# A parallel attention and MLP kernel: the first 512 tokens' second products of two pairs in one sum, and a subtract in two halves

## The chip, the cores and the metric

The kernel runs on one core of one Trainium2 chip. The metric is device time in microseconds (us) of one execution. An execution of the kernel before is 713.65 us (median of three runs, 713.02 to 713.98).

## The reference

`x` has 2048 tokens of 640 features. The output is the sum of three branches, two of which work on the layer-normed input:

```python
xn = _layernorm(x, axis=-1)
return x + _A_ref(xn, A_wqkv, A_w_phi, A_wo) + _B_ref(xn, B_w1, B_b1, B_w2, B_b2)
# A: 32 heads of 20; softmax features of q and k, linear attention, @ wo
# B: y = _layernorm(x); h = _gelu(y @ w1 + b1)   (F = 1728);  h @ w2 + b2
```

The change lies in branch B, the MLP.

## The kernel before, in words

All data is float32. For TensorE each operand is split exactly into a high and a low part of type float32r, and a product is three matmuls (`mm3`, L69 to L72): high by high (L70), high by low (L71), low by high (L72). The weights are the first operand, so L72 needs the low part of the weights and L71 the low part of the tokens or of the hidden layer.

Tokens are handled in four blocks of 512 (block 0 to 3), features in 5 chunks of 128 (`KC`), the hidden layer in 14 chunks of 128, which are taken in 7 pairs. For a pair and a block, `Mlp.passes` makes the *first products* (y by w1, per chunk of the pair, 5 `mm3` each), GELU and the split of the hidden layer, and then the *second products*: for each of 5 output chunks `m`, two `mm3` (one for each chunk of the pair) into a bank of PSUM, and one addition on VectorE of this bank into `acc[b]` (L329 for pair 0, which adds the bias b2 too; L331 for the others). The bank comes from `self.po`, which goes round banks 5, 6 and 7; bank 3 and 4 (`self.px`) are for side work. TensorE can write a bank again only when VectorE's addition has read it.

Work that is not the MLP's is put between the matmuls by hand. Each `mm3` ends with `self.tick()`, which runs the steps that are due (`self.after(ticks, step)`) and takes one step of a generator `mlp.beside`. On VectorE, ScalarE (ACT), GpSimd (POOL) and TensorE the order of the instructions is the order in which the code issues them (`manual_schedule`) in the two stages that matter here; each engine works its own queue in order.

The **first stage** (L523 to L696): pair 0's first products of block 0 are made in half blocks while the tokens still arrive. Then come the first products of pair 1 in block 0, the second products of pair 0 (`p00`) and those of pair 1 (`p10`); after `p10`'s third and fourth addition `products` (L640) puts a batch of four small matmuls (shown as eight L644) between. Beside it `next_y` (L651) splits w2 of pair 1 (L671: ACT makes the high part at L61, GpSimd the low part at L64) and makes the normalized tokens of block 1: GpSimd subtracts the mean (L680), VectorE scales (L682), ACT makes the high part (L684), VectorE the low part (L686). The first products of block 1 need these.

The **later stage** (L1358 to L1383): for blocks 2 and 3 the pairs 1 to 5 use a scheme of seven products instead of eight (`cross`), which needs sums of weight blocks. `sums` (L380) makes them on GpSimd, 768 columns (`s`), and `splits` (L406) splits them into high and low: ACT copies `s` (L392), and one tick later VectorE subtracts (L393, 128x768). The five uses of it are called the first to the fifth split here; the second to fifth are issued in the loop at L1377 to L1380, while `second` (L334) makes the second products of block 2. The low part is used by the next pair's `cross`. On VectorE's queue stand there also: `second`'s additions into `acc` (L342), the low part of the hidden layer (L461), the attention's additions (L1228) that free banks 3 and 4 for the attention's products (L1214, L1215), and shuffles (L1263). GpSimd has subtracts for the other weights (L393, 128x640), for the attention's features (L1208) and products for the attention's quotients (L1265).

Of the kernel before, what the change touches and what calls it, by code (L numbers as in the profile page):

```python
# [9 lines left out]
F32R = mybir.dt.float32r  # L10
AF = mybir.ActivationFunctionType
ALU = mybir.AluOpType
# [3 lines left out]
P = 128  # L16
S, D, F, H, DH = 2048, 640, 1728, 32, 20
KC = D // P
# [28 lines left out]
def f(ap):  # L47
    return ap.bitcast(F32)
# [3 lines left out]
def tile_kernel(ctx: ExitStack, tc: tile.TileContext, x, xT, wkT, wqT, wv, wphi, wo, w1, b1, w2, b2,  # L52
                ident, mmask, emask, vsel, out):
    nc = tc.nc
# [14 lines left out]
    def mm3(ps, lh, ll, rh, rl, first, last, **kw):  # L69
        nc.tensor.matmul(ps, lh, rh, start=first, stop=False, **kw)  # L70
        nc.tensor.matmul(ps, lh, rl, start=False, stop=False, **kw)  # L71
        nc.tensor.matmul(ps, ll, rh, start=False, stop=last, **kw)  # L72
# [6 lines left out]
    b2t = cp.tile([P, KC], F32, name="b2t")  # L79
# [18 lines left out]
    acc = [None] * NB  # L98
# [21 lines left out]
    def mtile(i, dtype=F32):  # L120
        return mp.tile([P, 2, D if i < 5 else 512], dtype, name=f"m{i}")
# [92 lines left out]
    class Mlp:  # L214
# [74 lines left out]
        def passes(self, g, b, ws, hid=None):  # L289
# [27 lines left out]
            for m in range(KC):  # L317
# [13 lines left out]
                    nc.vector.tensor_tensor(acc[b][:, m, :], pw, acc[b][:, m, :], op=ALU.add)  # L331
                yield

        def second(self, g, b, w, hid):  # L334

            for m in range(KC):
                pw = self.po()
                ms = slice(m * P, (m + 1) * P)
                for j, (hh, hl) in enumerate(hid):
                    mm3(pw, w[:, 2 * j, ms], w[:, 2 * j + 1, ms], hh, hl, j == 0, j == 1)  # L340
                    self.tick()
                nc.vector.tensor_tensor(acc[b][:, m, :], pw, acc[b][:, m, :], op=ALU.add)  # L342
                yield

        def fetch_pair(self, g, second):

            r1 = rp.tile([P, D], F32, name="r1")
            r2 = rp.tile([P, D], F32, name="r2")
            self.raw[g, second] = r1, r2
            for c, r in ((2 * g, r1), (2 * g + 1, r2)):  # L350
                n = min(P, F - c * P)
                if second:
                    for o in range(0, P, n):
                        nc.sync.dma_start(r[o:o + n, :], w2[c * P:c * P + n, :])
                else:
                    nc.sync.dma_start(r.rearrange("p (c f) -> p c f", f=P)[:, :, 0:n], w1[c, :, :, 0:n])
# [49 lines left out]
        def splits(self, g):  # L406

            raw, sums = self.weights(g)
            r1, r2 = self.raw.pop((g, False))
            s = self.raw.pop((g, "s")).rearrange("p i q f -> p (i q f)")  # L410
            return [lambda: self.split(raw[0][:, 0], raw[0][:, 1], r1), lambda: self.split(sums[:, 0], sums[:, 1], s, nc.vector),
                    lambda: self.split(raw[1][:, 0], raw[1][:, 1], r2)]

        def cross(self, g, bs, before, later):
# [102 lines left out]
    mlp = Mlp((0, 1, 2, 3), ((0, 2), (1, 3)))  # L517

    def finish(p):
        for _ in p:  # L520
            pass
# [6 lines left out]
    wc, parts, dmas = {}, {}, {}  # L528
# [8 lines left out]
    gts = mtile(4)  # L537
    hid = [mtile(2 * j + 1, F32R) for j in range(2)]
    hid = [(h[:, 0, :512], h[:, 1, :512]) for h in hid]
# [67 lines left out]
    next(rows1)  # L607
    for c in range(2):
        parts[c][1](nc.vector)
    p00 = mlp.passes(0, 0, [wc[0], wc[1]], hid)  # L610
    next(p00)

    rs = ExitStack()
    fp = rs.enter_context(tc.tile_pool(name="prep", bufs=2, reuse_waits="tile"))
# [25 lines left out]
    def products(us, raw):  # L640
        ps = mlp.px()
        for u, (n, g, i) in enumerate(us):
            nh = 6 if g < 5 else 4
            nc.tensor.matmul(ps[:, u * nh * DF:(u + 1) * nh * DF], raw[:nh * DH, u * P:(u + 1) * P], wpt[:nh * DH, g, :nh, 1:],  # L644
                             start=True, stop=True)
        return us, ps
# [40 lines left out]
            yield  # L687

    mlp.beside = next_y()
    p10 = mlp.passes(1, 0, [wc[2], wc[3]])  # L690
    next(p10)
    finish(p00)
    for m, _ in enumerate(p10):
        if m in (2, 3):
            first_done.append(products(jobs[0][m - 2], first_raws[m - 2]))
    finish(mlp.beside)  # L696
# [154 lines left out]
    for g in range(2, 7):  # L851
        for b in range(2):
            if b == 0:
                ws, wn = wn, []
# [162 lines left out]
    for t, i in [(t, i) for t in range(14) for i in range(4)] + TAIL:  # L1017
        if (t, i) in ((4, 0), (8, 0)):
            b = t // 4 + 1
# [33 lines left out]
        if (t, i) == (11, 0):  # L1053
            mlp = Mlp((0, 3, 2, 1), ((1, 2), (0, 3)))
# [16 lines left out]
    def pairs(w1t, w2t):  # L1071

        return [(*(w1t[:, 2 * j + p].rearrange("p (c f) -> p c f", f=P) for p in range(2)), w2t[:, 2 * j], w2t[:, 2 * j + 1])
                for j in range(2)]

    ws = pairs(w1t, w2t)
# [256 lines left out]
    at = {}  # L1333
# [36 lines left out]
    for g in range(1, 6):  # L1370
        w2t, later = gathered(g)
        hid, more = mlp.cross(g, (2, 3), before, later)
# [19 lines left out]
    ws = pairs(w1t, w2t)  # L1392
# [17 lines left out]
    for b in range(NB):  # L1410
        oh, ol = at[b].oh, at[b].ol
        for m in range(KC):
            ms = slice(m * P, (m + 1) * P)

            for cols in [slice(0, 512)] if (b, m) != (NB - 1, KC - 1) else [slice(0, 256), slice(256, 512)]:
                pw = pw_()[:, cols]
# [72 lines left out]
```

## Time and profile before

| | |
|---|---|
| three runs | 713.02, 713.65 and 713.98 us |
| the profiled execution | 713.46 us, of which its span (first to last instruction) is 711.6 us |
| TensorE (PE) | 703.8 us busy, 99% |
| weight loads (PEld) | 592.2 us |
| VectorE (DVE) | 514.0 us, 72% |
| GpSimd (POOL) | 421.4 us, 59% |
| ScalarE (ACT) | 342.0 us, 48% |
| granted TensorE clock | 1.000 over the span |
| moved by DMA | 106.56 MB, 149 GB/s over the span |

Rows in time order give the start in us from the span's start, the duration in us, the engine, the line of the kernel, the operation, what it writes and reads by the program's names, the shape, and in brackets the idle time of the engine before it and what ended it. A matmul's row is longer than the distance to the next one's start, since matmuls are pipelined. Names lose their numbers in the profile: `bank` is any PSUM bank, `m` any of the scratch tiles, `w` any weight tile.

### The profile page before, as it was taken

To read this page: it belongs to the slowest core of one execution; us is meant where nothing else is said; L and a number is where in the kernel's file an instruction comes from. 1 tells how busy PE (TensorE), PEld (TensorE's weight loads), DVE (VectorE), ACT (ScalarE), POOL (GpSimd) and SP (SyncE) were. 2 spreads that over 40 slices of the span, in tenths; PEclk is the share of its full clock that TensorE was granted. 3 is DMA by queue.
4 is the path that set the end of the run, shared out by engine and by line. 5 is a ranking of instruction groups with operands and counts; after the bars stand their busy time and mean duration, and the time that the engine had idled before them with its cause. 6 is when DMAs were issued, how large, how long until landed. Compare 5 with 4: busy or idle time off the path is not lost. (4 is left out here: it accounts for less than half of the span.)

```text
span 711.6 us, 9745 instructions
## 1 busy us (share of the span) xinstructions
PE 703.8 (99%) x3381; PEld 592.2 (83%) x3381; DVE 514.0 (72%) x821; ACT 342.0 (48%) x563; POOL 421.4 (59%) x360
## 2 busy tenths in 40 slices
PE   9999999999999999999999999999999999999998
PEld 7878888888888888888888888888887878888886
DVE  7777755988754788788888878657769695784622
ACT  6434554444334545545544546367665766450100
POOL 3521314577245997898787879468679787540400
PEclk9999999999999999999999999999999999999999
DMA  9823643485621228236401609964355568446222
GB/s 325 288 72 109 193 121 98 155 266 172 214 105 74 93 75 245 70 110 199 99 0 32 159 1 349 227 191 127 115 162 153 164 187 296 164 127 214 84 80 74
DMA packets 65767, 106.56 MB, mean 150 GB/s; under 512 B 7462, under 2 KB 31814, under 8 KB 63838
## 3 DMA queue, kind: packets, MB, share of 16 engines
q1 hardware_dynamic: 65414, 105.93, 46.5%
q8 instruction: 26, 0.43, 0.2%
q14 instruction: 23, 0.19, 0.1%
q10 hardware_dynamic: 304, 0.01, 0.0%
HBM read 71.37 MB, written 34.55 MB: 149 GB/s over the span
## 5 line engine op out<-in xcount | busy, mean ns | idle before, releaser
L906 PE MATMUL bank<-wkh,y 128*128 128x512 f32 (+1 forms) x480 | 139.5, 364 | 0.0
L70 PE MATMUL bank<-y,w 128*128 128x512 f32 (+1 forms) x294 | 114.2, 389 | 0.0
L71 PE MATMUL bank<-y,w 128*128 128x512 f32 (+1 forms) x294 | 113.7, 387 | 0.0
L72 PE MATMUL bank<-y,w 128*128 128x512 f32 (+1 forms) x294 | 113.6, 386 | 0.0
L64 POOL TENSOR_TENSOR w<-r,w 128x640 fp32r<-128x640 f32 x32 | 52.2, 1645 | 96.0 <-ACT w L61 67.0
L70 PE MATMUL bank<-m,w 128*128 128x512 f32 x260 | 102.3, 394 | 1.1 <-DVE acc L331 0.8
L71 PE MATMUL bank<-m,w 128*128 128x512 f32 x260 | 101.3, 390 | 0.9 <-DVE m L461 0.9
L72 PE MATMUL bank<-m,w 128*128 128x512 f32 x260 | 101.3, 390 | 0.0
L906 PEld LDWEIGHTS bank<-wkh,y 128*128 128x128 f32 x480 | 87.5, 188 | 13.3
L906 PE MATMUL bank<-wkl,y 128*128 128x512 f32 (+1 forms) x240 | 87.4, 364 | 0.0
L70 PEld LDWEIGHTS bank<-y,w 128*128 128x128 f32 x294 | 55.2, 188 | 11.7 <-issue 0.4
L72 PEld LDWEIGHTS bank<-y,w 128*128 128x128 f32 x294 | 55.2, 188 | 11.3
L71 PEld LDWEIGHTS bank<-y,w 128*128 128x128 f32 x294 | 55.2, 188 | 10.9
L942 ACT ACTIVATE m<-m,rs_all 128x1280 f32<-128x1280 f32 x32 | 43.7, 1365 | 42.9 <-POOL m L941 42.8
L70 PEld LDWEIGHTS bank<-m,w 128*128 128x128 f32 x260 | 48.8, 188 | 11.9 <-DVE acc L331 1.0
L944 DVE TENSOR_REDUCE sm<-m 128x64 f32<-128x1280 f32 x32 | 47.4, 1481 | 15.0 <-ACT m L942 14.8
L71 PEld LDWEIGHTS bank<-m,w 128*128 128x128 f32 x260 | 48.8, 188 | 11.1 <-DVE m L461 1.4
L906 PE MATMUL bank<-w,y 128*128 128x512 f32 x240 | 57.4, 391 | 0.0
L72 PEld LDWEIGHTS bank<-m,w 128*128 128x128 f32 x260 | 48.8, 188 | 10.2
L941 POOL TENSOR_TENSOR m<-m,mx 128x640 f32<-128x640 f32 (+2 forms) x48 | 44.4, 939 | 19.2 <-DVE mx L930 19.2
L331 DVE TENSOR_TENSOR acc<-bank,acc 128x512 f32<-128x512 f32 x70 | 46.9, 683 | 11.1 <-PE bank L72 5.9
L906 PEld LDWEIGHTS bank<-w,y 128*128 128x128 f32 x240 | 44.4, 188 | 8.5
(184 smaller groups left out, 1447.2 us busy)
## 6 DMA issues: line engine op xcount, KB each, us to landing
r<-in_w SPq DMA_DIRECT2D x52, 320.0 KB
e<-e SPq DMA_DIRECT2D x40, 256.0 KB
e<-acc SPq DMA_DIRECT2D x52, 160.0 KB
acc<-in_xT SPq DMA_DIRECT2D x4, 1280.0 KB
t<-t SPq DMA_DIRECT2D x8, 512.0 KB
tf<-t SPq DMA_DIRECT2D x2, 1536.0 KB
xb<-in_x SPq DMA_DIRECT2D x8, 320.0 KB
t<-in_x SPq DMA_DIRECT2D x8, 320.0 KB
```

The costliest lines, as they stand in the source:

```text
L64: eng.tensor_tensor(lo, src, f(hi), op=ALU.subtract)
L70: nc.tensor.matmul(ps, lh, rh, start=first, stop=False, **kw)
L71: nc.tensor.matmul(ps, lh, rl, start=False, stop=False, **kw)
L72: nc.tensor.matmul(ps, ll, rh, start=False, stop=last, **kw)
L331: nc.vector.tensor_tensor(acc[b][:, m, :], pw, acc[b][:, m, :], op=ALU.add)
L906: nc.tensor.matmul(ps, lh[:, kc, c], rh[:, kc], start=n == 0, stop=n == 3 * KC - 1)
L941: subs[n, t] = nc.gpsimd.tensor_tensor(ep[:, s], a, b, op=ALU.subtract)
L942: exps[n, t] = nc.scalar.activation(e, e, AF.Exp, scale=rs_all[:, t:t + 1])
L944: nc.vector.tensor_reduce(sm, e.rearrange("p s (h f) -> p (s h) f", f=DH), axis=AX, op=ALU.add)
```

## The change

Two edits. First, block 0's second products of pairs 0 and 1 are no longer two passes with ten additions. A new method `firsts` makes pair 1's first products, and `seconds` sums both pairs in one bank per output chunk, with one addition (with bias) each, five in all. Pair 0's products for the first three chunks go to the three banks first; then, chunk by chunk, pair 1's products are added in the same bank. The two batches of `products` stay behind the third and fourth addition. Second, in `splits` the subtract that makes the low part of the sums is issued in two halves of 384 columns, one tick and three ticks after ACT's copy.

```diff
+        def firsts(self, g, b, ws):
+            self.turn ^= 1
+            hid, gts = [], mtile(4)
+            for j, w in enumerate(ws):
+                hs = mtile(self.hid[self.turn][j], F32R)
+                hid.append((hs[:, 0, :512], hs[:, 1, :512]))
+                self.first(g, j, b, w, gts[:, j, :512], *hid[-1])
+            return hid
+
+        def seconds(self, b, *pairs):
+            def products(m, n):
+                ws, hid = pairs[n]
+                ms = slice(m * P, (m + 1) * P)
+                for j, (w, (hh, hl)) in enumerate(zip(ws, hid)):
+                    mm3(pw[m], w[2][:, ms], w[3][:, ms], hh, hl, (n, j) == (0, 0), (n, j) == (1, 1), skip_group_check=True)
+                    self.tick()
+
+            pw = [self.po() for _ in range(3)]
+            for m in range(3):
+                products(m, 0)
+            for m in range(KC):
+                if m > 2:
+                    pw.append(self.po())
+                    products(m, 0)
+                products(m, 1)
+                nc.vector.scalar_tensor_tensor(acc[b][:, m, :], pw[m], b2t[:, m:m + 1], acc[b][:, m, :], op0=ALU.add, op1=ALU.add)
+                yield
...
-            return [..., lambda: self.split(sums[:, 0], sums[:, 1], s, nc.vector),
+            def sum_parts():
+                nc.scalar.activation(sums[:, 0], s, AF.Copy)
+                for i, ticks in enumerate((1, 3)):
+                    at = slice(3 * P * i, 3 * P * (i + 1))
+                    self.after(ticks, lambda at=at: nc.vector.tensor_tensor(sums[:, 1, at], s[:, at], f(sums[:, 0, at]), op=ALU.subtract))
+
+            return [..., sum_parts,
...
-    p00 = mlp.passes(0, 0, [wc[0], wc[1]], hid)
-    next(p00)
+    mlp.turn ^= 1
...
-    p10 = mlp.passes(1, 0, [wc[2], wc[3]])
-    next(p10)
-    finish(p00)
-    for m, _ in enumerate(p10):
+    hid = [hid, mlp.firsts(1, 0, [wc[2], wc[3]])]
+    for m, _ in enumerate(mlp.seconds(0, ([wc[0], wc[1]], hid[0]), ([wc[2], wc[3]], hid[1]))):
```

What it moves on the engines is shown at three places, in the program's order (bank number and buffer number stand behind a name; `w0` to `w3` are the weights of the four hidden chunks, `m0` to `m3` their hidden layer).

TensorE in block 0, from pair 0's sum for the third chunk (bank 7) to pair 1's first sum. Before:

```order
L72 MATMUL bank7_481<-m3_151,w1_173 128x512
L70 MATMUL bank5_489<-m1_150,w0_172 128x512 [waits DVE_49]
...
L72 MATMUL bank6_499<-m3_151,w1_173 128x512
L70 MATMUL bank7_511<-m0_390,w2_174 128x512 [waits DVE_49,Activation_49]
L71 MATMUL bank7_511<-m0_390,w2_174 128x512
L72 MATMUL bank7_511<-m0_390,w2_174 128x512 [waits Pool_49]
```

and now:

```order
L72 MATMUL bank7_463<-m3_151,w1_173 128x512
L70 MATMUL bank5_461<-m0_390,w2_174 128x512 [waits Activation_49]
L71 MATMUL bank5_461<-m0_390,w2_174 128x512 [waits DVE_49]
L72 MATMUL bank5_461<-m0_390,w2_174 128x512 [waits Pool_49]
L70 MATMUL bank5_461<-m2_440,w3_175 128x512 [waits Activation_49]
L71 MATMUL bank5_461<-m2_440,w3_175 128x512 [waits DVE_49]
L72 MATMUL bank5_461<-m2_440,w3_175 128x512 [waits Pool_49]
```

Pair 1's second products, with their waits for ACT's and GpSimd's parts of w2, have moved up by two sums (12 matmuls), and the waits for VectorE's release of a bank ahead of them are gone.

VectorE in block 0, from the first addition on. Before:

```order
L329 SCALAR_TENSOR_TENSOR acc0_103<-bank5_489,b2t_61,acc0_103 128x512
L682 TENSOR_TENSOR xb_493<-xb_493,m5_415 128x512
L329 SCALAR_TENSOR_TENSOR acc0_103<-bank6_499,b2t_61,acc0_103 128x512
L682 TENSOR_TENSOR xb_503<-xb_503,m5_415 128x512
L686 TENSOR_TENSOR y11_148<-xb_493,y01_147 128x512
L331 TENSOR_TENSOR acc0_103<-bank7_511,acc0_103 128x512
L682 TENSOR_TENSOR xb_515<-xb_515,m5_415 128x512
L686 TENSOR_TENSOR y11_148<-xb_503,y01_147 128x512
L331 TENSOR_TENSOR acc0_103<-bank5_524,acc0_103 128x512
```

and now (the lines are numbered anew: L361 is the addition, L717 and L721 are L682 and L686 of before):

```order
L361 SCALAR_TENSOR_TENSOR acc0_103<-bank5_461,b2t_61,acc0_103 128x512
L717 TENSOR_TENSOR xb_489<-xb_489,m5_415 128x512
L361 SCALAR_TENSOR_TENSOR acc0_103<-bank6_462,b2t_61,acc0_103 128x512
L717 TENSOR_TENSOR xb_498<-xb_498,m5_415 128x512
L721 TENSOR_TENSOR y11_148<-xb_489,y01_147 128x512
L361 SCALAR_TENSOR_TENSOR acc0_103<-bank7_463,b2t_61,acc0_103 128x512
L717 TENSOR_TENSOR xb_509<-xb_509,m5_415 128x512
L721 TENSOR_TENSOR y11_148<-xb_498,y01_147 128x512
L717 TENSOR_TENSOR xb_527<-xb_527,m5_415 128x512
```

The three additions of pair 0 that stood ahead of these rows are gone, and so are two of the later ones; the work on block 1's tokens keeps its order.

VectorE at the fifth split. Before:

```order
L1228 TENSOR_TENSOR acc0_5165<-bank4_5422,ts_5166 64x512
L393 TENSOR_TENSOR w2_4360<-s_5379,w2_4360 128x768
L1263 STREAM_SHUFFLE rx_4376<-rx_4376 128x512
L342 TENSOR_TENSOR acc2_4122<-bank5_5432,acc2_4122 128x512
L1263 STREAM_SHUFFLE rx_4376<-rx_4376 128x512
L342 TENSOR_TENSOR acc2_4122<-bank6_5447,acc2_4122 128x512
L461 TENSOR_TENSOR m2_5403<-m6_5211,m2_5403 128x512
L1228 TENSOR_TENSOR acc0_5165<-bank3_5452,ts_5166 64x512
```

and now (L445 is the subtract, L1296 the shuffle, L372, L497 and L1261 are L342, L461 and L1228 of before):

```order
L1261 TENSOR_TENSOR acc0_5159<-bank4_5416,ts_5160 64x512
L445 TENSOR_TENSOR w2_4350<-s_5373,w2_4350 128x384
L1296 STREAM_SHUFFLE rx_4367<-rx_4367 128x512
L372 TENSOR_TENSOR acc2_4112<-bank5_5426,acc2_4112 128x512
L445 TENSOR_TENSOR w2_4350<-s_5373,w2_4350 128x384
L1296 STREAM_SHUFFLE rx_4367<-rx_4367 128x512
L372 TENSOR_TENSOR acc2_4112<-bank6_5441,acc2_4112 128x512
L497 TENSOR_TENSOR m2_5397<-m6_5205,m2_5397 128x512
L1261 TENSOR_TENSOR acc0_5159<-bank3_5447,ts_5160 64x512
```

The second half stands behind one shuffle and one addition, still ahead of the hidden layer's subtract and of the attention's addition. At the third and fourth split the second half likewise stands behind one or two additions and ahead of the next L461; at the first split both halves stand next to each other.

More of the change, by code (lines that the diff above doesn't have):

```diff
@@ L410, in splits @@
             s = self.raw.pop((g, "s")).rearrange("p i q f -> p (i q f)")
[L411 removed]
+            def sum_parts():
[3 more added lines that the diff above has]
+                    self.after(ticks, lambda at=at: nc.vector.tensor_tensor(sums[:, 1, at], s[:, at], f(sums[:, 0, at]), op=ALU.subtract))
+            return [lambda: self.split(raw[0][:, 0], raw[0][:, 1], r1), sum_parts,
                     lambda: self.split(raw[1][:, 0], raw[1][:, 1], r2)]
```

## The prediction

> **What bounds the kernel now.** I read the page first, then TensorE's waits, then the time-ordered rows of TensorE, VectorE and GpSimd at each wait. The page's busy line says how little there is to win:
>
> ```profile
> span 711.6 us, 9745 instructions
> PE 703.8 (99%) x3381; PEld 592.2 (83%) x3381; DVE 514.0 (72%) x821; ACT 342.0 (48%) x563; POOL 421.4 (59%) x360
> ```
>
> TensorE is the bound and idles 7.8 us of 711.6. VectorE and GpSimd have slack on average, but only single places count. TensorE's table of waits names them (in total, times, longest):
>
> ```profile
> PE bank L71 <- DVE m L461: 0.9, 1, 0.9
> PE bank L70 <- DVE acc L331: 0.8, 1, 0.8
> PE bank L1214 <- DVE acc L1228: 0.6, 1, 0.6
> ```
>
> The middle one lies in the first stage, at the second products of pairs 0 and 1. The other two lie behind the 768-wide subtracts that the second edit cuts in two. TensorE's rows around the middle one (start, us, instruction, idle before):
>
> ```profile
> 30.72 0.40 PE L70 MATMUL bank<-m,w 128*128 128x512 f32 x1
> ...
> 35.97 0.39 PE L72 MATMUL bank<-m,w 128*128 128x512 f32 x1
> 36.50 0.50 PE L70 MATMUL bank<-m,w 128*128 128x512 f32 x1
> ...
> 37.99 1.04 PE L644 MATMUL bank<-wpt,raw 120*128 120x114 f32 x8
> 39.83 0.50 PE L70 MATMUL bank<-m,w 128*128 128x512 f32 x1 [0.79 <-DVE acc L331]
> ...
> 41.32 1.04 PE L644 MATMUL bank<-wpt,raw 120*128 120x114 f32 x8
> 42.13 0.48 PE L70 MATMUL bank<-m,w 128*128 128x512 f32 x1
> ```
>
> Look at starts, not at ends: the 24 matmuls from 30.72 to 35.97 start 0.228 us apart. The next was due at 36.20, came at 36.50, and lasted 0.50 instead of 0.39, which the one behind it lost as well: 0.30 + 0.11 = 0.41. The eight L644 and the change back to 512 columns take 0.81 undisturbed (41.32 to 42.13), so behind those of 37.99 the next product was due at 38.80; it came at 39.83, 1.03 late. **1.44 us** is lost here. Why, VectorE's and GpSimd's rows tell:
>
> ```profile
> 34.03 1.75 DVE L682 TENSOR_TENSOR xb<-xb,m 128x512 f32<-128x512 f32 x1 [0.97 <-POOL xb L680]
> 35.71 0.74 DVE L329 SCALAR_TENSOR_TENSOR acc<-bank,b2t,acc 128x512 f32<-128x512 f32 x1
> ...
> 39.09 0.68 DVE L331 TENSOR_TENSOR acc<-bank,acc 128x512 f32<-128x512 f32 x1
> ...
> 45.58 0.67 DVE L686 TENSOR_TENSOR y<-xb,y 128x512 fp32r<-128x512 f32 x1
> ```
>
> ```profile
> 29.63 3.12 POOL L64 TENSOR_TENSOR w<-r,w 128x640 fp32r<-128x640 f32 x2 [4.41 <-ACT w L61]
> 32.70 7.60 POOL L680 TENSOR_TENSOR xb<-acc,m 128x512 f32<-128x512 f32 x5
> ```
>
> VectorE's adds that free a bank (L329, L331) take 0.68 to 0.74, also at 39.09, while GpSimd works. Its 128x512 instructions with both operands in SBUF (L682, L686, L461) take 0.67 alone (45.58) and 1.75 under GpSimd's (34.03): they take turns with it. So the adds queue behind stretched neighbours, and the banks come free late.
>
> **Edit one: block 0 in one sum.** Removed: five L331 adds; all 60 matmuls and both L644 batches stay. The old waits for banks go: a bank is written again only after 18 matmuls or more, where two sums (12) lay between before. But pair 1's products start where pair 0's fourth sum stood, at 30.72, and no longer at 33.47. They need the low part of pair 1's w2, which GpSimd makes in the two L64 rows above, 29.63 to 32.75, not driven by TensorE and so not moved. Pair 1's third matmul wants the first of them (ends 31.20) at 31.17: about 0.08 late. Its sixth, due at 31.94, wants the second, 32.75: with the 0.06 that lies between a VectorE add's end (39.77) and TensorE's restart (39.83) it starts at 32.81, 0.87 late, and the restart costs 0.11. New loss **1.06**.
>
> Behind it, does VectorE keep up? The first add runs at about 33.3, before L682 at 34.03; the second takes the slot of the old 35.71 and ends at 36.45; the bank it frees is wanted only about 40.3. Two L331 fewer stand ahead of the last L686 (old 45.58), which block 1's fifth first product needs; it comes near 44.6, TensorE asks near 46.0. The first L644 batch moves up from 37.99 to about 35.9; I cost its two tiles at nothing, since TensorE waited for no transfer anywhere (a late one would show as a wait for a DMA in the table above). So edit one gives 1.44 − 1.06 = **−0.4 us**. Bounds: −1.44 if GpSimd's wait were free, 0 if a second such wait followed. The two L64 are quoted, so −0.4 is nearest. The three banks' rotation shifts by one place for the rest of the stage, with as many matmuls between two uses as before: nothing.
>
> **Edit two: halves.** Five times one subtract of 768 columns becomes two of 384, the second two ticks of the scheduler (two matmul groups) later. The row by source of the old form (minimum, median, maximum ns):
>
> ```profile
> L393 DVE TENSOR_TENSOR w<-s,w x5: 1218/2045/2050, 454.5 to 575.2; 128x768 fp32r<-128x768 f32 x5
> ```
>
> Its work is estimated at 0.87 (0.67 for 512 columns, 45.58, with starts 0.60 apart), so every one of the five waited for GpSimd, up to 1.2. A half works about 0.47; two halves cost 0.07 more than one whole, and the second takes a turn of its own. Nobody waits for the low part itself: the next group's products use it several us later. What matters is what stands behind it on VectorE. I replay the rows with one rule read off them: who finds the other at work starts when that one ends, and at such an end the one that has waited goes first.
>
> Third split (rows of VectorE, GpSimd, TensorE):
>
> ```profile
> 516.07 0.68 DVE L342 TENSOR_TENSOR acc<-bank,acc 128x512 f32<-128x512 f32 x1
> ...
> 518.67 0.70 DVE L461 TENSOR_TENSOR m<-m,m 128x512 fp32r<-128x512 f32 x1
> ...
> 519.90 1.40 DVE L1228 TENSOR_TENSOR acc<-bank,ts 64x512 f32<-64x512 f32 x2
> ```
>
> ```profile
> 515.30 2.28 POOL L393 TENSOR_TENSOR w<-r,w 128x640 fp32r<-128x640 f32 x1
> 517.54 1.30 POOL L1208 TENSOR_TENSOR e<-e,m 128x512 fp32r<-128x512 f32 x1
> 518.78 1.75 POOL L1208 TENSOR_TENSOR e<-e,ph 128x512 fp32r<-128x512 f32 x1
> ```
>
> ```profile
> 521.62 0.39 PE L1214 MATMUL bank<-m,kvs 128*128 128x512 f32 x1
> ```
>
> The whole subtract got its turn at 515.30 and ended 0.77 later, at 516.07. Half one ends at 515.68; GpSimd's L393 then runs its 1.47 (516.07 to 517.54) to 517.15; half two, queued behind one add, waits for that and ends at 517.54. GpSimd is back on its old times, VectorE is not: L1228, a reciprocal and L342 took 2.00 (516.67 to 518.67) and bring L461 to 519.54, where it finds the second L1208 at work until 519.99. It ends at 520.51, the add behind it at 521.11, L1228 at 521.78. TensorE wants that bank at 521.62 (before, the first of the two L1228 ended at 520.57): 0.22 late and 0.11 restart, **+0.3**.
>
> Fourth split, the wait of L71:
>
> ```profile
> 548.66 1.29 DVE L342 TENSOR_TENSOR acc<-bank,acc 128x512 f32<-128x512 f32 x2
> 549.86 1.83 DVE L461 TENSOR_TENSOR m<-m,m 128x512 fp32r<-128x512 f32 x1
> ```
>
> ```profile
> 549.87 1.28 POOL L1265 TENSOR_TENSOR acc<-acc,rx 128x512 f32<-128x512 f32 x1
> ```
>
> ```profile
> 551.75 0.50 PE L71 MATMUL bank<-m,w 128*128 128x512 f32 x1 [0.95 <-DVE m L461]
> ```
>
> L461 asked within 0.01 of GpSimd's start and had to wait its 1.23 out; TensorE lost 1.22 (due 550.64; restart included). In the new order both halves still stand ahead of it, the second in the place of the second L342. All behind half one comes 0.40 earlier: half two asks at 548.86, gets its turn at 549.47 (549.87 − 0.40) and ends at 549.86. GpSimd's L1265 then runs until about 551.08; L461 asks at 550.46, behind the moved add, and ends near 551.6 as before: **0.0**.
>
> Fifth split, the wait of L1214:
>
> ```profile
> 577.76 0.75 DVE L1263 STREAM_SHUFFLE rx<-rx 128x512 f32<-128x512 f32 x1
> ...
> 578.98 0.69 DVE L461 TENSOR_TENSOR m<-m,m 128x512 fp32r<-128x512 f32 x1
> 579.59 0.67 DVE L1228 TENSOR_TENSOR acc<-bank,ts 64x512 f32<-64x512 f32 x1
> ```
>
> ```profile
> 577.82 1.30 POOL L1265 TENSOR_TENSOR acc<-acc,rx 128x512 f32<-128x512 f32 x1
> 579.08 1.72 POOL L1208 TENSOR_TENSOR e<-e,ph 128x512 fp32r<-128x512 f32 x1
> ```
>
> ```profile
> 580.32 0.50 PE L1214 MATMUL bank<-m,kvs 128*128 128x512 f32 x1 [0.63 <-DVE acc L1228]
> ```
>
> Before, L461 asked at 578.98, 0.10 ahead of GpSimd's end at 579.08, and did not wait. With halves, the first ends 0.40 earlier, and both queues with it: the second half stands where the shuffle did and asks at 577.36, GpSimd's L393 ends at 577.42 (577.82 − 0.40), half two at 577.81. GpSimd's L1265 takes 1.26 alone (577.82 to 579.08) and about 1.20 when it has waited (the L1208 of 518.78 ran from L461's end near 519.3 to 520.5), so it ends between 579.01 and 579.07; the shuffle and an add (1.22) bring L461 to 579.03. The margin of 0.10 has become −0.02 to +0.04. The nearest row is the fourth split's (0.01, lost), so I take it as lost: L461 waits for L1208 until 580.26, L1228 ends at 581.45, TensorE restarts at 581.51 instead of 580.32: **+1.2**. Ends: +0.1 if L461 wins, +1.2 if it loses. The first two splits give nothing: in the second, the replay leaves the bank's add 0.7 before its use, in the first GpSimd is idle.
>
> Turns as such are also a rule of the Trainium skill, "SBUF — State Buffer", section "Who interferes with whom": a VectorE instruction with two SBUF inputs and a GpSimd instruction that reads SBUF exclude each other for a whole instruction, and issue order decides who blocks. It speaks against this edit, which asks for the lock twice. By it the sum is the one here; with shares of bandwidth instead of turns each split would cost its 0.07 alone, and the sum would be edit one's, 713.1. The fourth split's pair of rows (1.83 beside 1.28) agrees with the rule.
>
> **Sum:** −0.4 + 0.3 + 0.0 + 1.2 = +1.1 us. The profiled execution took 713.46 (span 711.6 and 1.9 around it), 0.2 under the median of the three runs, 713.65, and inside their 713.02 to 713.98. So 714.5.
>
> **Rivals.**
> - *The race at the fifth split is won* (+0.1 instead of +1.2): sum 0.0, 713.5. For it: before, a margin of 0.10 was enough. Against: the margin is now nil, and at 0.01 the fourth split lost. 27%.
> - *A further turn is lost, slower than before*: at the third split L461 asks at 519.54 and GpSimd's boundary is 519.99. If VectorE runs over 0.44 later there, GpSimd starts its next L1208 first, L461 waits 1.25 more, and the bank at 521.62 comes 1.1 later still than in the sum: +2.2, 715.7. For it: VectorE has no idle time there in which to catch up. Against: 0.44 is more than any step of the replay is uncertain by. 21%, together with an equal loss at the fourth.
> - *The halves let the awaited instructions through*: an order of turns that I did not foresee takes away the losses of the fourth split (1.22) and the fifth (0.90: due 579.53, came 580.32, restart 0.11). −0.4 − 1.22 − 0.90 = −2.5, 711.0; with the fourth alone 711.8. For it: before, the fourth was lost by 0.01. Against: the program's order leaves both halves ahead of the awaited subtract. 20%, of which 3 end just within the bound (the third split's +0.3 and the won race's +0.1 beside the fourth's 1.22: 712.2).
>
> **How the numbers follow.** My forecast has 32%. About 0.2% (1.43 us, 712.2 to 715.1) is what a measurement of this kernel can tell from no change. Forecast, first rival and 3 of the third make 62% within it, 17% faster, 21% slower. The range of 8 in 10 holds the forecast, the won race, the further turn and the edge of the third rival: 712.1 to 715.9. The forecast with the won race alone: 713.2 to 714.9.
>
> **What would show it.** Right: a wait of TensorE for GpSimd's w L64 of 0.9 near 32, no wait for L331 in block 0, block 1's first product near 43.2. Right for the halves: near 579 L461 above 1.7 us, and L1214's wait near 1.8; a short wait of L1214 near 521.6; the wait of L71 at 551 unchanged. Wrong: no wait near 32, or the waits at 551 and 580 gone. All times in the later stage are to be read 0.4 earlier.

## The result and the profile after

The changed kernel takes **716.42 us** (median of 8 runs, 715.34 to 717.81), the kernel before 713.87 (8 runs, 712.35 to 714.91): ratio 1.0038, 95% interval 1.0025 to 1.005. It is about 2.6 us slower. The forecast was 714.5, the range ended at 715.9.

The profiled execution of the changed kernel took 715.63, 2.17 more than that of before. The page's head:

```profile
span 713.9 us, 9745 instructions
PE 704.3 (99%) x3381; PEld 591.3 (83%) x3381; DVE 515.1 (72%) x821; ACT 341.8 (48%) x563; POOL 420.0 (59%) x360
```

The busy time of TensorE grew by 0.5 of the 2.3 us that the span grew; the rest is idle time. TensorE's table of waits (in total, times, longest; a row of 0.2 that both kernels have is left out):

```profile
PE bank L1247 <- DVE acc L1261: 1.8, 1, 1.8
PE bank L614 <- POOL m L612: 1.3, 1, 1.3
PE bank L181 <- DVE xb L172: 0.9, 2, 0.5
PE bank L71 <- DVE m L497: 0.9, 1, 0.9
PE bank L72 <- POOL w L64: 0.5, 1, 0.5
PE bank L70 <- DVE acc L331: 0.5, 1, 0.5
```

The lines have moved: L1247, L1261 and L497 are the old L1214, L1228 and L461; L445 is the half subtract, L372 the old L342, L1241 and L1298 are GpSimd's old L1208 and L1265 (the experiments' lines differ by a few again). The 1.3 us of L614 are the first wait of the kernel, and stand before too (L578). The wait for GpSimd's w L64 is new, the one at the fifth split has grown from 0.6 to 1.8. The same in TensorE's rows, in time order:

```profile
31.18 0.39 PE L71 MATMUL bank<-m,w 128*128 128x512 f32 x1
31.50 0.50 PE L72 MATMUL bank<-m,w 128*128 128x512 f32 x1
...
32.07 0.40 PE L71 MATMUL bank<-m,w 128*128 128x512 f32 x1
33.00 0.50 PE L72 MATMUL bank<-m,w 128*128 128x512 f32 x1 [0.53 <-POOL w L64]
...
43.39 0.39 PE L70 MATMUL bank<-y,w 128*128 128x512 f32 x1
...
153.79 0.39 PE L72 MATMUL bank<-m,w 128*128 128x512 f32 x1
154.64 0.50 PE L70 MATMUL bank<-m,w 128*128 128x512 f32 x1 [0.46 <-DVE acc L331]
...
522.22 0.39 PE L72 MATMUL bank<-m,w 128*128 128x512 f32 x1
522.60 0.50 PE L1247 MATMUL bank<-m,kvs 128*128 128x512 f32 x1
...
551.54 0.39 PE L70 MATMUL bank<-m,w 128*128 128x512 f32 x1
552.81 0.50 PE L71 MATMUL bank<-m,w 128*128 128x512 f32 x1 [0.88 <-DVE m L497]
...
580.36 0.39 PE L72 MATMUL bank<-y,w 128*128 128x512 f32 x1
582.55 0.50 PE L1247 MATMUL bank<-m,kvs 128*128 128x512 f32 x1 [1.79 <-DVE acc L1261]
```

Read the distance between two starts: undisturbed it is 0.227. Matched one by one with the matmuls of before, the starts lose 0.24 in the first 20 us, gain 0.45 in block 0 (block 1's first product at 43.39, before at 43.60), lose 0.77 at 154, 0.20 more at 169 and 194, 0.36 up to and at the third split (522.60), gain 0.07 at the fourth (the wait at 552 is there in both), and lose 1.15 at the fifth (582.55). These sum to 2.20. At the fifth split VectorE's and GpSimd's rows are:

```profile
576.27 0.82 DVE L445 TENSOR_TENSOR w<-s,w 128x384 fp32r<-128x384 f32 x1
...
578.40 0.55 DVE L445 TENSOR_TENSOR w<-s,w 128x384 fp32r<-128x384 f32 x1
...
580.10 1.79 DVE L497 TENSOR_TENSOR m<-m,m 128x512 fp32r<-128x512 f32 x1
581.82 0.67 DVE L1261 TENSOR_TENSOR acc<-bank,ts 64x512 f32<-64x512 f32 x1
```

```profile
578.47 1.64 POOL L1298 TENSOR_TENSOR acc<-acc,rx 128x512 f32<-128x512 f32 x1
580.06 1.28 POOL L1241 TENSOR_TENSOR e<-e,ph 128x512 fp32r<-128x512 f32 x1
```

L497 stands behind the second half, comes to its start at 580.10, just as GpSimd has started L1241 (580.06), waits it out and takes 1.79 instead of the 0.69 of before; the bank's add L1261 and with it TensorE come late by as much. So this one execution follows the forecast's steps. But it is among the quickest of the 8, and two questions stay: the 0.97 at 154 to 194, which no step foresaw, and the median, 0.8 above this execution.

### The profile page after: what moved, and what is told of

Read it like the earlier page. It is cut to its first block, busy times and chain, and to the rows that moved or that the text cites. A ratio compares the mean times of both kernels' runs of the same rounds, so it can differ in the third digit from the quotient of the medians.

```text
span 713.9 us, 9745 instructions
## 1 busy us (share of the span) xinstructions
PE 704.3 (99%) x3381; PEld 591.3 (83%) x3381; DVE 515.1 (72%) x821; ACT 341.8 (48%) x563; POOL 420.0 (59%) x360
## 5 line engine op out<-in xcount | busy, mean ns | idle before, releaser
L71 PE MATMUL bank<-y,w 128*128 128x512 f32 (+1 forms) x294 | 113.7, 387 | 0.0
L64 POOL TENSOR_TENSOR w<-r,w 128x640 fp32r<-128x640 f32 x32 | 52.1, 1644 | 96.9 <-ACT w L61 68.3
L71 PE MATMUL bank<-m,w 128*128 128x512 f32 x260 | 101.3, 390 | 0.9 <-DVE m L497 0.9
L71 PEld LDWEIGHTS bank<-y,w 128*128 128x128 f32 x294 | 55.2, 188 | 10.9
L71 PEld LDWEIGHTS bank<-m,w 128*128 128x128 f32 x260 | 48.8, 188 | 11.0 <-DVE m L497 1.3
L331 DVE TENSOR_TENSOR acc<-bank,acc 128x512 f32<-128x512 f32 x65 | 43.6, 684 | 10.6 <-PE bank L72 5.4
```

The source lines that it names most:

```text
L64: eng.tensor_tensor(lo, src, f(hi), op=ALU.subtract)
```

## The experiments

Each kernel was timed in five rounds beside the kernel before on the same chip. The three sets of runs of before have medians of 713.99 (35 runs; it belongs to the first four experiments), 714.12 (34; the next four) and 713.74 (20; the last four).

**Edit one alone.** The subtract is whole again:

```diff
-            return [lambda: self.split(raw[0][:, 0], raw[0][:, 1], r1), sum_parts,
+            return [lambda: self.split(raw[0][:, 0], raw[0][:, 1], r1), lambda: self.split(sums[:, 0], sums[:, 1], s, nc.vector),
```

> The change's first edit alone (block 0 in one sum; the subtract of the sums whole, as before). Theory T (turns): the change is slower by my own terms, edit one -0.4 us and edit two +1.5 us (third split +0.3, fifth +1.2), and the profile of the changed kernel has 0.9 us more between 150 and 195 us that are scatter of single executions. It expects this kernel 0.4 us under the kernel before (0.3 to 0.6), a wait of TensorE for GpSimd's w near 32 us, and the waits at 550 (1.2) and 579 us (0.9) as before. Rival S (shift): the 0.9 us between 150 and 195 us belong to edit one, because TensorE and VectorE come earlier to transfers that do not; it expects this kernel 0.5 us or more over the kernel before, with a wait for a bank near 154 us in the profile.

Measured: 713.2 (712.31 to 713.99, 11 runs), ratio 0.9986 (0.9974 to 0.9997), 0.8 below before. The trace has the wait for w L64 (0.5) and smaller ones near 154 and 194. Block 0 is 0.42 us shorter in it than in the trace of before. Edit one gains, and the whole loss is edit two's. The forecast's −0.4 lies inside the interval, which reaches from −1.9 to −0.2 us.

**Edit two alone.** The old block 0, the halves kept:

```diff
-    mlp.turn ^= 1
+    p00 = mlp.passes(0, 0, [wc[0], wc[1]], hid)
+    next(p00)
...
-    hid = [hid, mlp.firsts(1, 0, [wc[2], wc[3]])]
-    for m, _ in enumerate(mlp.seconds(0, ([wc[0], wc[1]], hid[0]), ([wc[2], wc[3]], hid[1]))):
+    p10 = mlp.passes(1, 0, [wc[2], wc[3]])
+    next(p10)
+    finish(p00)
+    for m, _ in enumerate(p10):
```

> The change's second edit alone (both passes of block 0 as before, the subtract of the sums in two halves). Theory T: +1.5 us against the kernel before; in block 0 the two old waits (1.4 us), a short wait near 521.8 us (0.3) and a wait of L1214's kind at 580 us of 2.1 instead of 0.9 us. Rival S: also +1.5, its difference lies in the first edit. A third theory, that a half more costs only its 0.07 us of extra work, expects 0.0 to +0.1.

Measured: 716.95 (715.27 to 718.33, 12 runs), ratio 1.0038 (1.0026 to 1.005), 3.0 above before, twice the 1.5 that theory T expected. The losses near 154 and 194 are in this trace too, with the old block 0: they are not edit one's. At 154 they go with a transfer. ACT's copy of `t` (the old L782) stands idle for 1.35 to 1.40 us ahead of its start in the five traces without the loss (before, the late half, the earlier w2, the fifth split alone, three additions at the addition waited for), and for 2.1 to 3.0 in the nine with it; in eight of these nine, as in the five, the row names a DMA, `t<-t`. VectorE's subtract and the addition L331 behind it come late by this, so TensorE's row names VectorE. Why the transfer comes late was not followed. And something new stands behind the wait at the fifth split. TensorE's rows there:

```profile
580.96 0.39 PE L72 MATMUL bank<-y,w 128*128 128x512 f32 x1
583.14 0.50 PE L1220 MATMUL bank<-m,kvs 128*128 128x512 f32 x1 [1.79 <-DVE acc L1234]
583.47 0.58 PE L1221 MATMUL bank<-e,kvs 128*128 128x512 f32 x1
583.86 0.63 PE L70 MATMUL bank<-y,w 128*128 128x512 f32 x1
584.28 0.63 PE L71 MATMUL bank<-y,w 128*128 128x512 f32 x1
...
586.42 0.63 PE L70 MATMUL bank<-m,w 128*128 128x512 f32 x1
586.84 0.44 PE L71 MATMUL bank<-m,w 128*128 128x512 f32 x1
587.12 0.40 PE L72 MATMUL bank<-m,w 128*128 128x512 f32 x1
```

From 583.86 to 586.84 the starts lie 0.43 apart instead of 0.227, with nothing waited for. The view by stretches names the cause; its first number behind POOL's brackets is the granted clock, first in this kernel:

```profile
582.00:584.00 2.00, 0.86 (x3) 0.73 (x4) 2.00 (x5) 0.00 (x0) 1.62 (x1) 0.88 0.70 187
584.00:586.00 2.00, 2.00 (x7) 1.52 (x6) 1.90 (x5) 0.59 (x1) 1.38 (x2) 0.50 0.46 49
586.00:588.00 2.00, 2.00 (x8) 1.63 (x7) 1.88 (x4) 0.00 (x0) 1.19 (x1) 0.77 0.90 344
```

and then in the changed kernel's profiled execution, behind a wait just as long:

```profile
582.00:584.00 2.00, 1.45 (x6) 1.24 (x7) 1.97 (x5) 0.60 (x1) 1.20 (x2) 1.00 0.27 104
584.00:586.00 2.00, 2.00 (x10) 1.65 (x10) 1.93 (x5) 0.18 (x1) 1.79 (x2) 1.00 0.83 211
```

With halves the clock fell to 0.50, and 0.12 + 0.50 + 0.23 of the three stretches of 2 us is 1.7 us of full clock lost, about 1.6 of which the starts show. In the changed kernel's profiled execution it did not fall. Over a span of 716 a loss of 1.7 us is a mean clock of 0.998, which every run lists: 4 of the 8 runs of the changed kernel have 0.998 (716.49 to 717.81), the four others 0.999 or 1.0 (715.34 to 716.36); the two medians lie 1.5 us apart. The 89 runs of before and the 11 of edit one alone are all at 0.999 or above.

**The second half later.** Six ticks behind the copy, behind the subtract and the add that TensorE waits for:

```diff
-                for i, ticks in enumerate((1, 3)):
+                for i, ticks in enumerate((1, 6)):
```

> The changed kernel with the second half six ticks behind ACT's copy instead of three: at every split of the later stage it then stands behind the hidden layer's second subtract, and at the fifth behind the attention's addition too. Theory T (what costs is the second turn ahead of an instruction that TensorE waits for): the added waits at the third and fifth split go, and since only half of the subtract stands ahead, the fifth's wait falls under the 0.9 us of before, to about 0.5; 1.5 to 1.9 us under the changed kernel, 0.2 to 1.0 over the kernel before if S holds, 0.8 under it if not. Rival H (the halves cost by their number, wherever they stand): as the changed kernel, 2.5 over the kernel before.

Measured: 713.75 (712.73 to 715.29, 12 runs), ratio 0.9998 (0.9986 to 1.001). The fifth split's big wait and the fourth's are gone. The kernel is 2.7 us under the changed one, more than the 1.5 to 1.9 that theory T expected: so much hangs on where the second half stands. The 0.5 us above edit one alone cannot be told from chance.

**Edit one with an earlier w2.** Pair 1's second weights are split ahead of its GELUs:

```diff
+        for c in range(2, 4):
+            parts[c][1]()
         for st in (s23, s47):
             step(st, 1)
         for _ in range(4):
             yield
...
-        for c in range(2, 4):
-            parts[c][1]()
```

> Edit one alone, with the split of pair 1's w2 (ACT's two copies and GpSimd's two subtracts) issued 8 steps earlier, ahead of pair 1's GELU. Theory T: the wait of TensorE for GpSimd's w near 32 us goes, and with it 1.1 us against edit one alone: 1.4 us under the kernel before. Rival S adds its 0.9 to both. A rival for this place: ACT's two copies delay pair 1's GELU, so that TensorE waits for the hidden layer instead and gains under 0.5 us.

Measured: 712.56 (711.92 to 714.08, 11 runs), ratio 0.9978 (0.9967 to 0.999). The wait for w L64 is gone, but a wait as long stands in its place, for VectorE's low part of the hidden layer (VectorE's, then GpSimd's, then TensorE's rows):

```profile
29.90 0.86 DVE L698 TENSOR_TENSOR wpt<-wpt 120x684 f32<-120x684 f32 x1
30.68 1.78 DVE L64 TENSOR_TENSOR m<-m,m 128x512 fp32r<-128x512 f32 x1
```

```profile
30.63 2.98 POOL L709 TENSOR_TENSOR xb<-acc,m 128x512 f32<-128x512 f32 x2 [1.27 <-DMA m<-r]
```

```profile
32.52 0.50 PE L71 MATMUL bank<-m,w 128*128 128x512 f32 x1 [0.54 <-DVE m L64]
```

Against edit one alone block 0 is 0.24 us shorter in the traces, not 1.1; the 0.6 us between the two medians cannot be told from chance. So the median lies where theory T had it, 1.4 below before, but not for its reason.

**Halves at the fifth split alone.**

```diff
             def sum_parts():
+                if g != 5:
+                    return self.split(sums[:, 0], sums[:, 1], s, nc.vector)
```

> The changed kernel with the sums' low part made in two halves at the fifth split alone (near 576 us), whole at the four others. Reference: edit one alone, 713.2. Theory: the cost of the halves sits mostly at the fifth split, in two terms: TensorE's wait there grows from 0.63 to about 2.0 us (+1.2 on the path, as between the traces of edit one alone and of the changed kernel), and after a wait of some 2 us the granted clock halves for 3.4 us in about half of the executions (+1.55 in those, +0.75 on the median): 715.2, the trace with a wait of 1.8 to 2.1 us of the matmul of the queries behind L1261 near 580, and a mean granted clock of 0.998 in about half of the timed runs. Rival: the 3.2 us between edit one alone and the changed kernel (716.42) is spread evenly over the five splits, 0.65 each: 713.9, no clock under 0.999.

Measured: 715.07 (713.21 to 716.74, 12 runs), ratio 1.0017 (1.0006 to 1.0027), 0.95 above before, so 1.75 above edit one alone. The wait at the fifth split is 1.8 us, as in the changed kernel; 4 of the 12 runs have a mean clock of 0.998. The cost is not spread evenly.

**Halves at the fourth split alone.** As above, with `g != 4`.

> The changed kernel with halves at the fourth split alone (near 546 us). Reference: edit one alone, 713.2, in whose trace TensorE doesn't wait near 551, while in those of before, of the changed kernel and of the halves alone it waits some 1.1 us there. Theory A: with the second half standing ahead of the hidden layer's low part (L497), that instruction always meets GpSimd's long one and the wait always comes: 714.2 to 714.4 and a wait of 1.0 to 1.2 us near 552. Theory B (the forecast's own term, 0.0): the wait near 551 comes or stays away by who is first at the port, whatever the halves do: 713.2 to 713.6. In both the clock stays, since the wait is 1.2 us and not 2.

Measured: 714.62 (713.22 to 715.27, 11 runs), ratio 1.0002 (0.9993 to 1.0011), 0.5 above before and 1.3 above edit one alone (resampling both sets and their runs of before gives 0.2 to 2.2); all clocks 0.999 or 1.0. Theory A holds: the wait of L71 is 0.9 us. VectorE's rows and one of GpSimd's in this kernel, then VectorE's in edit one alone:

```profile
549.23 1.08 DVE L447 TENSOR_TENSOR w<-s,w 128x384 fp32r<-128x384 f32 x1
550.23 0.68 DVE L372 TENSOR_TENSOR acc<-bank,acc 128x512 f32<-128x512 f32 x1
550.83 1.18 DVE L499 TENSOR_TENSOR m<-m,m 128x512 fp32r<-128x512 f32 x1
```

```profile
549.85 1.61 POOL L1300 TENSOR_TENSOR acc<-acc,rx 128x512 f32<-128x512 f32 x1
```

```profile
549.57 1.29 DVE L372 TENSOR_TENSOR acc<-bank,acc 128x512 f32<-128x512 f32 x2
550.77 0.68 DVE L491 TENSOR_TENSOR m<-m,m 128x512 fp32r<-128x512 f32 x1
```

The second half (L447) takes 1.08, and behind it the hidden layer's low part comes to its start at 550.83, in the midst of GpSimd's L1300, and takes 1.18; without it, it takes 0.68. Over all traces: with a second half ahead of that subtract (the changed kernel, halves alone, this one, both halves back to back) TensorE waits for it every time, 4 of 4; with a whole subtract or the late half there in 1 of 10, and that one is the profiled execution of before. In those ten VectorE's start lies 0.01 to 0.03 us ahead of GpSimd's, and 0.01 was lost in before (549.86 and 549.87) and won in edit one alone (550.77 and 550.78). But all nine that won have edit one in. Whether the kernel before loses there always or seldom isn't shown by its one trace.

**Three additions, at the wrong place.** Edit one alone, with one addition repeated:

```diff
+                for _ in range(3 if (self.b, g) == (2, 7) else 1):
-                nc.vector.tensor_tensor(o, pn[a, :], t, op=ALU.add)
+                    nc.vector.tensor_tensor(o, pn[a, :], t, op=ALU.add)
```

> Edit one alone with whole splits, and one addition of the attention's product (L1255, out of its bank, group 7 of block 2, near 579 us) made three times over, the same values each time: the bank comes free 1.36 us later (two additions of 0.68), and TensorE's wait at 580.09 grows from 0.63 to about 2.0 us without any halves. Theory: the length of TensorE's wait is what lowers the clock: 713.2 + 1.36 + about 0.75 on the median = 715.3, with a mean granted clock of 0.998 in about half of the runs and 0.5 for some 3.4 us behind the wait in those. Rival: the clock fell through the halves' own doings and a wait of 2 us costs its length alone: 714.6, the clock at 0.999 or above in all runs.

Measured: 715.16 (713.96 to 717.34, 12 runs), ratio 1.0013 (1.0 to 1.0026), all clocks 0.999 or 1.0. It does not test the theory: the repeated addition was the next one, so two waits came (1.4 together, the longer 0.8). It shows that two short ones leave the clock alone.

**Edit one, earlier w2, and the folded weights' subtract later.**

```diff
-        for _ in range(4):
-            yield
         nc.vector.tensor_tensor(wpt[:, :, :, 1:], wpt[:, :, :, 1:], wpt[:, :, :, 0:1].to_broadcast([G6, 6, 6, DF]), op=ALU.subtract)
+        for _ in range(4):
+            yield
```

(The four ticks taken away behind the subtract are those added ahead of it.)

> Edit one alone with pair 1's second weights split ahead of its GELUs, as in the run before it (712.56), and VectorE's subtraction on the folded weights (0.86 us near 29.9) moved four ticks later, behind both low parts of block 0's hidden layer. Theory: the wait of 0.81 us of TensorE near 31.6 came from that subtraction, which put the second low part (L64) into a turn with GpSimd's centering at 30.63; with it moved the low part starts near 29.9, beside no GpSimd instruction, and the wait goes: 711.8. Rival: the low part or the next instruction meets GpSimd all the same and the wait stays or moves to the first additions of block 0: 712.4 to 712.8.

Measured: 712.49 (710.84 to 713.84, 11 runs), ratio 0.9975 (0.9964 to 0.9986). The theory holds in block 0: no wait is left near 32, and block 0 is 1.08 shorter than with edit one alone (block 1's first product at 42.39, there at 43.28). The median is that of the kernel with the earlier w2 all the same: it lies where the rival had it, but not for the rival's reason. In the profiled execution, the slowest of the 11, the gain went at 465.72:

```profile
464.25 0.39 PE L70 MATMUL bank<-y,w 128*128 128x512 f32 x1
465.72 0.50 PE L71 MATMUL bank<-y,w 128*128 128x512 f32 x1 [1.09 <-DMA y<-t]
```

TensorE waits there for a transfer, for 1.09 us; of the other traces only that of both halves back to back has this wait. Whether the other runs have it was not measured, so it is open where the gain goes in the median. This version and the earlier w2 are about 1.5 us faster than before, and 4 than the changed kernel.

**Three additions, at the addition waited for.** As above, with group 6.

> As the run before with three additions, but at the addition that TensorE's wait near 580 really ends on (group 6 of block 2, 579.36 in the trace of edit one alone; the run before lengthened the next one, and gave two waits of 0.77 and 0.92 us). Whole splits, no halves. The one wait grows from 0.63 to about 2.0 us. Theory: the length of a single wait lowers the clock: 713.2 + 1.36 + about 0.75 on the median = 715.3, a mean granted clock of 0.998 in a third to half of the runs. Rival: the clock fell through the halves and not through the wait: 714.6, all runs at 0.999 or 1.0.

Measured: 716.18 (714.19 to 717.1, 9 runs), ratio 1.0029 (1.002 to 1.0039). The wait is 2.46 us, longer than the 2.0 expected; 8 of 9 runs have a mean clock of 0.998 (715.54 to 717.1), the ninth 1.0 and 714.19. There are no halves here: the rival falls. In the stretches 582 to 584 and 584 to 586 of its trace:

```profile
582.00:584.00 2.00, 2.00 (x7) 1.56 (x6) 1.90 (x5) 0.60 (x1) 1.36 (x2) 0.67 0.79 231
584.00:586.00 2.00, 2.00 (x6) 1.60 (x5) 1.80 (x4) 0.02 (x1) 1.21 (x1) 0.50 0.43 162
```

**Five additions.** The same with 5.

> The same with five additions: one wait of about 0.63 + 2.72 = 3.4 us at 580. Theory: the longer the wait, the more executions lose the clock; behind 3.4 us nearly all do: 713.2 + 2.72 + 1.55 = 717.5, a mean clock of 0.998 in most runs. Rival (the wait's length costs itself alone): 715.9, all runs at 0.999 or 1.0.

Measured: 717.94 (717.62 to 718.32, 5 runs), ratio 1.0055 (1.0042 to 1.0068); a wait of 3.59 us, and all 5 runs at 0.998 or below. The theory holds. One of the five has 0.995, about twice the loss of clock, and is no slower (718.01); no trace shows why.

**Halves at the first three splits alone.** With `g > 3` for a whole subtract.

> The changed kernel with halves at the first three splits alone (455, 485, 515 us), whole at the fourth and fifth. Reference: edit one alone, 713.2. Theory: these three cost what the forecast said, 0.3 at the third: 713.2 to 713.6; the sum of the three parts (this, 1.4 of the fourth, 1.9 of the fifth) then makes up the 3.2 us between edit one alone and the changed kernel. Rival: part of the cost sits here and the parts overlap: 714 or more.

Measured: 713.45 (712.31 to 714.66, 11 runs), ratio 0.9995 (0.9986 to 1.0004), 0.3 below before, 0.5 above edit one alone, within what the theory gives. Matched with before as above, its trace loses nothing at the first two splits and 0.31 at the third. Each against its own runs of before, 0.5 + 1.3 + 1.75 = 3.55 for the three parts stands beside 2.55 + 0.8 = 3.35 for edit two in the changed kernel: the costs add up, as far as their scatter of about 1 us each lets one say.

**Both halves back to back.**

```diff
-                for i, ticks in enumerate((1, 3)):
+                for i, ticks in enumerate((1, 1)):
```

> The changed kernel with both halves of the sums' low part standing one right behind the other at the place of the first, at all five splits. Theory (place decides): each half still takes its own turn beside GpSimd, but both lie where the whole instruction lay, ahead of an instruction that TensorE doesn't wait for at once; the low part of the hidden layer (L497) no longer stands behind a late half: 713.2 to 714.0. Rival (the number of turns decides, wherever they lie): about 716.4, as the changed kernel.

Measured: 719.36 (718.24 to 720.96, 6 runs), ratio 1.0079 (1.0066 to 1.0092). "Place decides", as it was put, falls, and the rival is outdone by 2.9 us. VectorE's rows at the second split show why, first in this kernel, with GpSimd's:

```profile
486.34 3.49 DVE L445 TENSOR_TENSOR w<-s,w 128x384 fp32r<-128x384 f32 x2
489.75 0.68 DVE L372 TENSOR_TENSOR acc<-bank,acc 128x512 f32<-128x512 f32 x1
```

```profile
485.82 1.75 POOL L1241 TENSOR_TENSOR e<-e,m 128x512 fp32r<-128x512 f32 x1
487.53 1.88 POOL L423 TENSOR_TENSOR w<-r,w 128x640 fp32r<-128x640 f32 x1
489.38 1.61 POOL L1241 TENSOR_TENSOR e<-e,m 128x512 fp32r<-128x512 f32 x1
```

and in edit one alone:

```profile
485.07 2.05 DVE L423 TENSOR_TENSOR w<-s,w 128x768 fp32r<-128x768 f32 x1
```

The whole subtract waits once and then does 768 columns; each half waits out one GpSimd instruction, and the pair takes 3.49 instead of 2.05. TensorE's wait at the fifth split is 2.6 us, 5 of 6 runs are at 0.998, and two waits of 0.9 and 0.8 stand at the fourth. (The profiled execution is the slowest of the six, 720.96; 1.1 of its waits is the transfer at 466.) What decides is how many times VectorE comes to its start while GpSimd is at work, and whether TensorE waits for what is queued behind. An add out of a bank between the halves, as in the changed kernel, hides a part of the second turn; the late half's turn hides behind the instructions that TensorE wants.

## Why the prediction was wrong

The sum's sign was right, its size was not: +2.55 in the medians where +1.1 stood, so 0.38% and not within the 0.2% to which the forecast gave most of the chance.

- *Edit one, −0.4.* Right. The wait for w L64 is where it was put (due 31.94, came 33.00: 1.06), block 0 gained 0.45 in the trace, block 1's first product stands at 43.39. The timed −0.8 agrees within its interval. One reading was off without consequence: the first bank is written again after 12 matmuls and one batch of L644, not after 18 or more; no wait for it is in the trace.
- *First two splits 0, third +0.3.* Right: 0.36 in the trace of after, 0.31 with halves at the first three alone (0.5 timed, with a scatter of about 1). Two readings were off: at the first split GpSimd is not idle (its L393 runs from 453.59 for 1.55, beside VectorE's at 454.54), though nothing waits there; and a half takes at least 0.55, not 0.47.
- *Fourth split 0.0.* **This step failed.** "L461 asks at 550.46 … and ends near 551.6 as before" took the loss of 1.22 in one profiled execution for a property of the kernel before. With a whole subtract or a late half it is a race, 0.01 to 0.03 us wide, that nine traces of ten show won; with the changed kernel's halves the subtract comes while GpSimd is at work, in every trace. In the comparison of the two profiled executions the step is 0.0, as forecast; against edit one alone, which won, it is about 1.3 in the medians. How much it is against the kernel before itself stays open, since the nine have edit one in: halves alone are 3.0 above before, and less 0.3 and 1.75 for the third and fifth split that leaves 0.95 for the fourth, with 0 to 1.5 within the interval. The changed kernel itself leaves about as much: 2.55 less the −0.45, 0.34 and 1.15 of the traces and the 0.5 of the clock (below) is 1.0. So it is likely, though not shown, that the kernel before seldom loses there. The rival of a further lost turn (715.7, with "an equal loss at the fourth" counted in) came nearest to the measured time, but it had its place at the third split, where nothing further was lost.
- *Fifth split +1.2.* Right on TensorE's path: the race was lost, the wait is 1.79, the starts lose 1.15. **Mis-sized, because a term was missing**: the wait is long enough to lower the granted clock in a third of the executions (11 of 32 with a wait of 1.8), which then costs about 1.6 more. 1.15 + 1.6 / 3 = 1.7; halves at the fifth split alone cost 1.75.
- *The base.* 713.46 was right as a time but mixed: that execution lost the fourth race (1.22) and had none of the losses at 154 to 194 (0.97 in after's trace, some in most others, with and without either edit). The two nearly cancel, which hid that such losses differ from one trace to the next. The loss at 154 also answers "a late one would show as a wait for a DMA in the table above": that transfer's lateness reaches TensorE through ACT and VectorE, and TensorE's table names VectorE's L331.
- *The range* was built from the turns alone. With the clock's 0.5 and the fourth split's 1.3 the forecast would have been 716.3.

The Trainium skill, "SBUF — State Buffer", section "Who interferes with whom", gives the two engines turns of a whole instruction: the back-to-back rows agree, 1.44 us more for the same columns in two instructions.

## What to carry to other kernels

In this kernel cutting an instruction in two gained nothing where it waits for turns with another engine: each piece waits for a turn, and what stands behind the second piece pays. A wait that one profiled execution shows may be a race; before it is counted as kept or won, ask by what margin it was lost and look at a second trace. A single idle stretch of TensorE near 2 us was worth more here than its length, in some executions.

## What the runs showed of the clock

A single wait of TensorE can lower its clock, with a chance that rises steeply with the length. Waits as the bracket in each kernel's one trace gives them, and timed runs with a mean clock of 0.998 or less:

| longest wait near 580 | kernels | runs at 0.998 or less |
|---|---|---|
| 0.4 to 0.8 us | before; edit one alone; late half; both with earlier w2; fourth alone; first three; additions at the wrong place | 0 of 168 |
| 1.8 us | the changed kernel, halves alone, fifth alone | 11 of 32 |
| 2.5 to 2.6 us | three additions, back to back | 13 of 15 |
| 3.6 us | five additions | 5 of 5 |

The clock falls 0.4 to 1.4 us behind the restart, to 0.50, and is back some 3.4 us later. In the four traces with a fall the loss is the same, about 1.6 us by TensorE's starts. Why one wait of 1.8 us lowers the clock and another does not, the traces' own record of the clock shows. All changes in a trace lie whole multiples of 3.413 us apart: with halves alone the first rise is at 6.66, the fall at 583.51, 169 multiples later, and the return at 586.93. So these marks, called bounds here, can be drawn near 580 from the first rise also where the clock did not fall:

| trace | wait | bound in it | longest part between two bounds | clock |
|---|---|---|---|---|
| fifth alone (first rise 5.54) | 578.33 to 580.12 | 578.98 | 1.14 | stays |
| the changed kernel (5.06) | 580.76 to 582.55 | 581.92 | 1.16 | stays |
| halves alone (6.66) | 581.35 to 583.14 | none | 1.79 | falls at the next bound, 583.51 |
| three additions (5.81) | 578.79 to 581.25 | 579.25 | 2.00 | falls at the next bound, 582.66 |
| back to back (7.28) | 583.62 to 586.24 | 584.13 | 2.11 | falls at the next bound, 587.54 |
| five additions (6.87) | 579.45 to 583.04 | 580.31 | 2.73 | falls at the next bound, 583.72 |

In these six traces the clock falls at the end of a stretch between two bounds in which TensorE waited for 1.79 us or more, and stays where it waited for 1.16 or less; where between them the limit lies they don't show. Since the bounds lie differently in each execution (the first rise at 4.67 to 7.37 us in the 14 traces), the same wait loses the clock in some and not in others. The Trainium skill, "TensorE: Matmul & The Clock Gate", Part 1, has the clock halve after an idle window of some 3.4 us, return after a busy one, and the window run freely: the return and the free-running window agree with these traces, but with halves alone the clock fell at the end of a window of which TensorE waited only 1.79 of 3.413 us.
